# Attention followed by a two-layer product: another order of the first two units' start

## The chip, the cores and the metric

The kernel runs on one core of one Trainium2 chip. The metric is the device time of one execution in microseconds; lower is better. A core has several engines that run beside one another, each with its own queue of instructions in program order: PE (TensorE, the matrix products), DVE (VectorE), ACT (ScalarE), POOL (GpSimd) and SP (SyncE, here only a queue for transfers). They wait for one another by semaphores. PE reads from the on-chip memory SBUF and writes into PSUM, eight banks of accumulators, from which DVE and ACT read.

## The reference

```python
scores = scale * q @ k.T          # 8 batches, 12 heads, 448 rows, 64 columns
attn = softmax(scores)            # with the row maximum taken off
x = attn @ v                      # heads put side by side: 3584 x 768
h = x @ w_in                      # 768 x 2048
g = maximum(0.01 * h, h)
out = g @ w_out                   # 2048 x 768
```

Inputs and output are float32. The kernel computes in bfloat16 with float32 accumulation, and leaves out the maximum, since the scores are small.

## The kernel before, in words

A unit is a pair of heads of one batch; there are 48. For each unit q and k are loaded, cast to bfloat16 (`cast`, into the buffer `qkb`), turned so that the head's columns lie on the partitions (`transposes` on PE, with a copy from PSUM into `qkT`), and multiplied to scores (`scores`). A unit's 448 keys are dealt with in four chunks of 112, so a unit has four calls of `scores`, each a pair of products (one for each head), and four calls of `expo`, the exponentials on ACT. `pv` multiplies the exponentials with v, one head at a time (16 small products), and divides by the sums on DVE; v carries a column of ones for them. `x_transposes` turns a unit's result for the big products.

Scores go to three PSUM slots of two banks each, in rotation (`next_slot`): a fourth score waits until the exponential of the first has read its slot. Everything else of this stage shares two banks, in rotation (`next_bank`).

The order is written out by hand. The program's order is each engine's order, and a scheduler doesn't change it. `first(u)` writes the order of the first six units (the first batch); after it, attention of later units is placed between the big products by a planner, which the change doesn't touch.

The start before: three loads on SP's queue (L217 to L219: k and q of unit 0, k of unit 1), in float32. All other loads go over POOL's queue and are cast to bfloat16 on the way. While the first two are under way, PE runs seven products of 128x512 on zeros (`warm_up`, L239), and DVE sets constants. k of unit 0 is cast by ACT and DVE together, one head each (`both`, L263), then q the same way. `transposes(0)` turns k first and q after it, in two tiles, each followed by five small products on zeros (`stay_warm`); ACT copies k out of PSUM, DVE copies q. Then DVE casts q and k of unit 1, and `first(0)` begins. In `first`, unit 0's and unit 1's fourth scores come late, after the next unit's transposes (unit 0) or between the two halves of unit 0's `pv` (unit 1). POOL casts v of unit 1 and everything from unit 3 on, by the lists in `supply`; its queue begins with the loads.

In the profile's rows L217 to L219 appear as L173 (the helper's line), casts as L190 (q, k) and L198 (v), L264 and L265 (unit 0's), `warm_up` as L241, `stay_warm` as L247, transposes as L301 and their copy as L305, scores as L319, exponentials as L331 and L334 (a unit's fourth chunk), `pv` as L362, L374 and L375, `x_transposes` as L389 and L390.

Of the kernel before, what the change touches and what calls it, by code (L numbers as in the profile page):

```python
# [16 lines left out]
def kernel(  # L17
# [48 lines left out]
    banks = [ps_g.tile([P, 4 * P], F32, name=f"g{i}") for i in range(2)]  # L66
# [7 lines left out]
    def next_bank():  # L74

        banks.reverse()
        return banks[1]
# [41 lines left out]
    h = h_pool.tile([P, MD, (KEEP + 1) * P], BF16, name="h")  # L119
    h_mix = h_pool.tile([P, MH, 2, P], BF16, name="hmix")  # L120
# [90 lines left out]
    def load_w(n=1):  # L211
        for _ in range(n):
            if w_steps:
                o, i = w_steps.pop(0)
                nc.gpsimd.dma_start(out=o, in_=i)

    load_one(0, 1, nc.sync)  # L217
    load_one(0, 0, nc.sync)
    load_one(1, 1, nc.sync)  # L219
    ident = const_pool.tile([P, P], BF16)  # L220
    make_identity(nc, ident)
# [6 lines left out]
    load_soft(5, 1, (2,))  # L228
    load_w(1)

    warm = h_mix.rearrange("p m c t -> p (m c t)")[:, :512]
    nc.vector.memset(warm, 0.0)

    word = const_pool.tile([P, 2], BF16)
# [2 lines left out]
    nc.scalar.copy(gate[:, :1], gate[:, 1:])  # L237

    def warm_up(n):  # L239
        for _ in range(n):  # L240
            nc.tensor.matmul(next_bank(), warm[:, :P], warm, start=True, stop=True)  # L241

    def stay_warm(n):

        ps = next_slot()
        for _ in range(n):
            nc.tensor.matmul(ps[:, 0, :P], warm[:, :P], warm[:, :P], start=True, stop=True)  # L247

    warm_up(7)
    nc.vector.memset(qkT_all.rearrange("p u i c s -> p u (i c s)")[:, :, 2 * S:2 * S + EP], 0.0)  # L250
    nc.vector.memset(v_old.rearrange("p u h so d -> p (u h so) d")[:, :, D:], 1.0)
    nc.vector.memset(e_all[:SC, :, EM:EM + EP], 0.0)
# [6 lines left out]
        nc.vector.memset(v_all[j * D:(j + 1) * D, :, 2 * KC + j, D:], 1.0)  # L259
    nc.vector.memset(e_all[:, :, EL:], 0.0)  # L260
    fast = nc.vector.tensor_copy

    def both(o, i):  # L263
        nc.scalar.copy(o[:, 0], i[:, 0])  # L264
        fast(o[:, 1], i[:, 1])  # L265

    cast(0, (1,), both)
    cast(0, (0,), both)


    x_t = {}
# [18 lines left out]
    def turn_tile(bank):  # L290
        bank = next_bank() if bank is None else bank
        return bank.bitcast(BF16)

    def transposes(u, bank=None):
        n = SC if u < HY else P
        t, flat = qkb[u % NB], qkT[u % NQ].rearrange("p i c s -> p (i c s)")[:, :2 * NSC * n]
        for parts in ((1,), (0,)) if u == 0 else ((0, 1),):
            tr = turn_tile(bank)[:, :2 * NSC * n].rearrange("p (i s) -> p i s", i=2)
            for i in parts:
                for so in range(NSC):  # L300
                    nc.tensor.transpose(tr[:, i, ts(so, n)], t[:n, i, so].rearrange("p h d -> p (h d)"), ident[:n, :n])  # L301
            if u == 0:
                stay_warm(5)
            at = slice(parts[0], parts[-1] + 1)
            (nc.scalar.copy if u == 0 and parts == (1,) else nc.vector.tensor_copy)(  # L305
                flat.rearrange("p (i s) -> p i s", i=2)[:, at], tr[:, at]
            )

    sc_t = {}

    def scores(u, c):
        ps = next_slot()
        t = qkT[u % NQ]
        sc_t[u, c] = ps
        if u < HY:
            t = t.rearrange("p i c s -> p (i c s)")
            for j in range(2):
                p = slice(j * D, (j + 1) * D)
                nc.tensor.matmul(ps[:, j, :S], t[p, S + c * SC:S + c * SC + P], t[p, :S], start=True, stop=True)  # L319
# [548 lines left out]
    def first(u):  # L868

        scores(u, 0)  # L870
        scores(u, 1)
        if u < 2:
            scores(u, 2)
        expo(u, 0)
        if u == 0:
            warm_up(1)
        expo(u, 1)
        if u >= 2:
            x_transposes(u - 2, next_bank())
        if u == 1:  # L880
            transposes(u + 1)
        if u >= 1:
            pv(u - 1, 0)
        if u > 1:
            scores(u, 2)
            scores(u, 3)
        if u != 1:
            transposes(u + 1)
        if u == 0:
            cast(2, (0, 1), fast)  # L890
            cast(0, (2,), fast)
# [12 lines left out]
    transposes(0)  # L904
    cast(1, (0, 1), fast)
    for u in range(HP):
        first(u)

# [78 lines left out]
    def turned(u):  # L987

        return u < to["pe"] or to["pe"] == NPE and u < to["turn"]
# [261 lines left out]
```

## Time and profile before

| | us |
|---|---|
| median of 3 runs (lowest, highest) | 377.68 (377.44, 377.75) |
| the profiled execution, its own time | 377.66 |
| its span, first to last instruction | 375.9 |
| PE busy | 369.2 (98%) |
| ACT busy | 259.7 (69%) |
| DVE busy | 256.7 (68%) |
| POOL busy | 190.6 (51%) |

The profile is one execution recorded by the hardware. A row of a timeline is: start, duration (both in us), engine, line, operation, what it writes and reads, the shape, how many instructions of the same kind were put together, and in brackets how long the engine had been idle before and which instruction ended that. "PEld" is PE's loading of weights, which overlaps its products. The end of a product is modelled: it includes the way through the array, so rows overlap, and the next row's start tells when the next product was issued. A row with several instructions begins with the first of them and lasts to the end of the last. The view of waits sums an engine's idle time by what it waited for: in total, how often, and the longest.

### The profile page before, as it was taken

How to read it: one execution, taken by the hardware profiler on the slowest of the kernel's cores; microseconds unless marked ns; L12 is line 12 of the kernel's file. 1: busy time of each engine (PE TensorE's matmuls, PEld its weight loads, DVE VectorE, ACT ScalarE, POOL GpSimd, SP SyncE). 2: the span in 40 equal slices, each digit the busy share in tenths (PEclk: the TensorE clock that was granted, in tenths of full speed). 3: DMA queues.
4: the chain of work that ended last, by engine and by line, in shares of the span. 5: the costliest groups of instructions: out<-in, count | busy, mean ns of one | idle time of the engine just before them, and what ended most of it. 6: DMA issues, size and time to landing. Idle time of an engine off the chain costs nothing.

```text
span 375.9 us, 10127 instructions
## 1 busy us (share of the span) xinstructions
PE 369.2 (98%) x4008; PEld 266.0 (71%) x4008; DVE 256.7 (68%) x559; ACT 259.7 (69%) x399; POOL 190.6 (51%) x376
## 2 busy tenths in 40 slices
PE   7899999999999999999999999999999999999996
PEld 4664658756698566996569966599665995679765
DVE  5665868778666867676676665875847775685754
ACT  6998895866768786758766587666787658626721
POOL 8976871985269969624488235792347020000000
PEclk9999999999999999999999999999999999999999
DMA  9999999999499966963969748798345740321123
GB/s 155 200 204 206 193 204 201 159 167 155 94 183 164 118 135 91 205 149 57 154 126 142 148 65 78 178 150 165 60 66 109 134 110 0 75 62 42 44 65 105
DMA packets 99920, 48.08 MB, mean 128 GB/s; under 512 B 64672, under 2 KB 96928, under 8 KB 99872
## 3 DMA queue, kind: packets, MB, share of 16 engines
q0 software_dynamic: 39600, 22.47, 44.4%
q1 hardware_dynamic: 60080, 24.84, 33.1%
q8 instruction: 31, 0.51, 0.6%
q14 instruction: 17, 0.14, 0.1%
q10 hardware_dynamic: 192, 0.12, 0.1%
HBM read 45.61 MB, written 11.01 MB: 151 GB/s over the span
## 4 chain that ended last, share of the span: by engine, by line
PE 96%; ACT 2%; DVE 1%; issue 0%; ACTq 0%
PE g L683 30%; PE g L548 14%; PE sc L548 14%; PE sc L322 7%; PE sc L350 6%; PE sc L319 4%; PE g L424 4%; PE sc L645 4%; PE sc L362 3%; PE g L821 2%; PE sc L343 2%; ACT e L331 2%; PE g L301 1%; PE g L362 1%; PE g L241 1%; PE sc L424 1%
## 5 line engine op out<-in xcount | busy, mean ns | idle before, releaser
L331 ACT ACTIVATE e<-sc 128x896 bf16<-128x896 f32 (+1 forms) x144 | 123.9, 930 | 30.4 <-PE sc L322 20.5
L683 PE MATMUL g<-w_out_sb,h 128*128 128x384 bf16 (+1 forms) x440 | 84.1, 326 | 0.0
L683 PEld LDWEIGHTS <-h 128*128 128x128 bf16 x592 | 54.3, 97 | 41.1 <-issue 10.8
L537 ACT ACTIVATE h<-c 128x512 bf16<-128x512 f32 (+1 forms) x72 | 43.1, 610 | 30.2 <-DVE c L563 12.4
L548 PEld LDWEIGHTS <-w_in_sb 128*128 128x128 bf16 x576 | 54.6, 98 | 5.8
L190 POOL COPY qkb<-fq 112x512 bf16<-112x512 bf16 x34 | 24.0, 705 | 43.5 <-DMA qkT<-qkb 34.5
L548 PEld LDWEIGHTS <-w_in_mix 128*128 128x128 bf16 x432 | 40.5, 98 | 3.7
L201 POOL COPY v<-fv 128x384 bf16<-128x384 bf16 x30 | 17.9, 596 | 44.2 <-PE sc L350 41.3
L688 DVE COPY o<-g 128x384 f32<-128x384 f32 x47 | 26.0, 553 | 13.6 <-PE g L683 13.5
L350 PE MATMUL sc<-v,e 128*128 128x65 bf16 x720 | 33.3, 194 | 0.0
L322 PE MATMUL sc<-qkT 64*128 64x448 bf16 (+1 forms) x210 | 32.8, 353 | 0.0
L350 PEld LDWEIGHTS <-e 128*128 128x128 bf16 x720 | 31.1, 98 | 1.3
L979 DVE RECIPROCAL rec<-sc 112x8 f32<-112x8 f32 x42 | 8.7, 207 | 33.9 <-PE sc L350 16.6
L980 DVE TENSOR_TENSOR x<-sc,rec 112x512 bf16<-112x512 f32 x42 | 29.0, 691 | 1.6 <-DVE rec L979 0.2
L548 PE MATMUL g<-xT,w_in_sb 128*128 128x256 bf16 (+1 forms) x216 | 28.5, 268 | 0.0
L548 PE MATMUL sc<-xT,w_in_sb 128*128 128x256 bf16 (+1 forms) x216 | 28.5, 268 | 0.0
L694 DVE TENSOR_TENSOR o<-o,g 128x384 f32<-128x384 f32 x39 | 21.5, 550 | 9.1 <-PE g L683 4.4
L343 PE MATMUL sc<-v,e 128*128 128x130 bf16 x120 | 26.5, 221 | 0.0
L649 DVE TENSOR_TENSOR o<-o,sc 128x192 f32<-128x192 f32 x39 | 13.7, 351 | 18.1 <-PE sc L645 18.1
L683 PE MATMUL g<-w_mix,h 128*128 128x384 bf16 x128 | 24.6, 327 | 0.0
L163 POOL DMA_DIRECT2D fv<-in_v_dram x32 | 20.1, 640 | 6.8 <-DMA fq<-in_q_dram 1.9
L683 PE MATMUL g<-w_mix,hmix 128*128 128x384 bf16 x112 | 21.7, 327 | 0.0
(149 smaller groups left out, 744.1 us busy)
## 6 DMA issues: line engine op xcount, KB each, us to landing
fq<-in_q_dram POOLq DMA_DIRECT2D x17, 224.0 KB, 5.7
w_out_sb<-in_moe_w_out_dram POOLq DMA_DIRECT2D x4, 768.0 KB, 13.2
out_dram<-o SPq DMA_DIRECT2D x7, 336.0 KB, 3.5
w_in_sb<-in_moe_w_in_dram POOLq DMA_DIRECT2D x2, 1152.0 KB, 12.9
out_dram<-o SPq DMA_DIRECT2D x7, 288.0 KB, 3.7
fk<-in_k_dram POOLq DMA_DIRECT2D x15, 128.0 KB, 6.0
fv<-in_v_dram POOLq DMA_DIRECT2D x15, 128.0 KB, 4.9
fk<-in_k_dram POOLq DMA_DIRECT2D x15, 96.0 KB, 6.1
```

The costliest lines, as they stand in the source:

```text
L163: nc.gpsimd.dma_start(out=t[p, :n, :, :so].rearrange("p u h so d -> p (u h) (so d)"), in_=(q, k, v)[x][b, hs, keys].rearrange("h (p so) d ...
L190: by(t[:SC, x].rearrange("p so h d -> p h so d"), f)
L322: nc.tensor.matmul(ps[:, j, :S].rearrange("p (so s) -> p so s", so=NSC), t[p, 1, c], t[p, 0, :, :SC], start=True, stop=True,)
L331: nc.scalar.activation(e[:, :, c, :], ps[:n, :, :S], AX.Exp, scale=scale)
L343: nc.tensor.matmul(ps, e[:, EM + qc * SC:EM + qc * SC + P], vt[:, 2 * KC:].rearrange("p j d -> p (j d)"), start=True, stop=False, skip_gro ...
L350: nc.tensor.matmul(ps[:, j * (D + 1):(j + 1) * (D + 1)], e[:, at:at + P], vt[:, j * KC + c], start=False, stop=(c == KC - 1), skip_group_c ...
L537: nc.scalar.activation(hs[:, m:m + 2, cols], x.rearrange("p (m t) -> p m t", m=2), AX.Prelu, alpha=0.01)
L548: nc.tensor.matmul(ps[:, j * nh:(j + 1) * nh], w[:, kk, ts(j, P)], x[:, kk], start=(first and j == 0 and kk == 0), stop=(kk == KH - 1), sk ...
L683: nc.tensor.matmul(ps[:, cols], x[:, m], w[:, m], start=(first and m == 0), stop=(m == MH - 1), skip_group_check=True,)
L688: by(o[:, at], ps[:, :NW])
L694: nc.vector.tensor_add(o[:, at], o[:, at], ps[:, :NW])
L980: nc.vector.tensor_mul(x, ps[:, :, :, :D], rec.to_broadcast([SC, 2, 2 * NP, D]))
```

## The change

- The loads of q and k of unit 0 change places on SP's queue.
- The warm-up on zeros is 26 products of 128x128 in place of 7 of 128x512, and the block of zeros is a quarter as wide. Between the first scores and the first slot's release there are 4 of them in place of 1 wide one.
- A new function `begin` casts, turns and copies unit 0. q first: DVE casts three of its four blocks, ACT the fourth, PE turns it in one tile. Of k, DVE casts the first block, ACT the other three; PE turns the first block alone in a tile of its own, then the other three in a third tile; DVE copies all three tiles. Two and three small products on zeros stand between.
- Of unit 0, the first chunk's scores use 112 columns of weights in place of 128, so that they read nothing of the second block.
- Unit 0's fourth scores come ahead of unit 1's transposes. Unit 1's fourth scores come ahead of both halves of unit 0's `pv`.
- Unit 1's k is cast before its q, and `transposes(1)` works in two tiles, k first, each with its own copy; unit 0's special case in `transposes` is gone.

```diff
+    load_one(0, 0, nc.sync)
     load_one(0, 1, nc.sync)
-    load_one(0, 0, nc.sync)
     load_one(1, 1, nc.sync)
...
-    warm = h_mix.rearrange("p m c t -> p (m c t)")[:, :512]
+    warm = h_mix.rearrange("p m c t -> p (m c t)")[:, :P]
...
     def warm_up(n):
-        for _ in range(n):
-            nc.tensor.matmul(next_bank(), warm[:, :P], warm, start=True, stop=True)
+        for x in range(n):
+            nc.tensor.matmul((next_bank() if x % 4 == 0 else banks[1])[:, :P], warm, warm, start=True, stop=True)
...
-    warm_up(7)
+    warm_up(26)
...
-    def both(o, i):
-        nc.scalar.copy(o[:, 0], i[:, 0])
-        fast(o[:, 1], i[:, 1])
-
-    cast(0, (1,), both)
-    cast(0, (0,), both)
...
-        for parts in ((1,), (0,)) if u == 0 else ((0, 1),):
+        for parts in ((1,), (0,)) if u == 1 else ((0, 1),):
...
+    def begin():
+
+        t, flat = qkb[0], qkT[0].rearrange("p i c s -> p (i c s)")
+
+        def turned(x, so):
+            tr = turn_tile(None)[:, :S]
+            for j in so:
+                nc.tensor.transpose(tr[:, ts(j, SC)], t[:SC, x, j].rearrange("p h d -> p (h d)"), ident[:SC, :SC])
+            at = slice(so[0] * SC, (so[-1] + 1) * SC)
+            return flat[:, x * S + at.start:x * S + at.stop], tr[:, at]
+
+        def copy(by, x, so):
+            by(t[:SC, x, so].rearrange("p so h d -> p h so d"), raw[0][x][:, :, so])
+
+        copy(nc.scalar.copy, 0, slice(3, 4))
+        copy(fast, 0, slice(0, 3))
+        copy(nc.scalar.copy, 1, slice(1, 4))
+        copy(fast, 1, slice(0, 1))
+        one = turned(0, range(NSC))
+        stay_warm(2)
+        fast(*one)
+        one = turned(1, range(1))
+        stay_warm(3)
+        fast(*one)
+        one = turned(1, range(1, NSC))
+        fast(*one)
...
+                n = SC if u == c == 0 else P
+                nc.tensor.matmul(ps[:n, j, :S], t[p, S + c * SC:S + c * SC + n], t[p, :S], start=True, stop=True)
...
         if u == 0:
-            warm_up(1)
+            warm_up(4)
+            scores(u, 3)
...
         if u == 1:
             transposes(u + 1)
+            scores(u, 3)
...
-        if u < 2:
-            scores(u, 3)
...
-    transposes(0)
-    cast(1, (0, 1), fast)
+    begin()
+    cast(1, (1, 0), fast)
```

More of the change, by code (lines that the diff above doesn't have):

```diff
@@ L246, in stay_warm @@
         for _ in range(n):
-            nc.tensor.matmul(ps[:, 0, :P], warm[:, :P], warm[:, :P], start=True, stop=True)
-    warm_up(7)
+            nc.tensor.matmul(ps[:, 0, :P], warm, warm, start=True, stop=True)
+    warm_up(26)
     nc.vector.memset(qkT_all.rearrange("p u i c s -> p u (i c s)")[:, :, 2 * S:2 * S + EP], 0.0)
@@ L301, in transposes @@
                     nc.tensor.transpose(tr[:, i, ts(so, n)], t[:n, i, so].rearrange("p h d -> p (h d)"), ident[:n, :n])
-            if u == 0:
-                stay_warm(5)
             at = slice(parts[0], parts[-1] + 1)
-            (nc.scalar.copy if u == 0 and parts == (1,) else nc.vector.tensor_copy)(
-                flat.rearrange("p (i s) -> p i s", i=2)[:, at], tr[:, at]
-            )
+            nc.vector.tensor_copy(flat.rearrange("p (i s) -> p i s", i=2)[:, at], tr[:, at])
+    def begin():
[20 more added lines that the diff above has]
+        fast(*one)
+        raw[0].clear() if len(raw[0]) == 2 else [raw[0].pop(x) for x in range(2)]
     sc_t = {}
@@ L318, in scores @@
                 p = slice(j * D, (j + 1) * D)
-                nc.tensor.matmul(ps[:, j, :S], t[p, S + c * SC:S + c * SC + P], t[p, :S], start=True, stop=True)
+                n = SC if u == c == 0 else P
+                nc.tensor.matmul(ps[:n, j, :S], t[p, S + c * SC:S + c * SC + n], t[p, :S], start=True, stop=True)
             return
```

## The prediction

> **What bounds the kernel now.** I read the page first, then PE's list of waits, then each engine's timeline over the first 26 us, because the whole change lies there.
>
> ```profile
> span 375.9 us, 10127 instructions
> PE 369.2 (98%) x4008; PEld 266.0 (71%) x4008; DVE 256.7 (68%) x559; ACT 259.7 (69%) x399; POOL 190.6 (51%) x376
> PEclk9999999999999999999999999999999999999999
> ```
>
> ```profile
> PE g L241 <- DVE gate L236: 1.2, 1, 1.2
> PE sc L319 <- DVE qkT L305: 0.6, 2, 0.4
> PE sc L319 <- ACT e L331: 0.6, 3, 0.2
> PE sc L319 <- ACT c L334: 0.4, 1, 0.4
> PE g L389 <- DVE x L375: 0.3, 1, 0.3
> ```
>
> These waits sum to 3.1 us, and the last of them ends at 21.99 (row below). From there PE has no recorded wait. A shift of PE's position at 22 us is therefore worth its full size at the end, and nothing after 22 us can give more. Before it, ScalarE's exponentials set the pace:
>
> ```profile
> 3.59 0.40 ACT L264 CAST qkb<-w_in_mix 112x256 bf16<-112x256 f32 x1 [1.36 <-DMA w_in_mix<-in_k_dram]
> 4.30 0.41 ACT L264 CAST qkb<-w_in_mix 112x256 bf16<-112x256 f32 x1 [0.31 <-DMA w_in_mix<-in_q_dram]
> 6.53 2.53 ACT L331 ACTIVATE e<-sc 112x896 bf16<-112x896 f32 x3 [1.22 <-PE sc L319]
> ...
> 12.92 2.59 ACT L331 ACTIVATE e<-sc 112x896 bf16<-112x896 f32 x3
> ...
> 16.11 2.63 ACT L331 ACTIVATE e<-sc 112x896 bf16<-112x896 f32 x3
> ```
>
> The first exponential starts at 6.53, the ninth (unit 2) at 12.92, the thirteenth (unit 3) at 16.11, with no idle bracket between: 9.58/12 = 0.80 us each. One lasts 2.53 - 2 x 0.80 = 0.93 and frees its slot at its end. So the question is how much earlier the first starts, and whether PE can follow that.
>
> **The start, term by term.** PE and VectorE before:
>
> ```profile
> 1.20 3.17 PE L241 MATMUL g<-hmix 128*128 128x512 bf16 x7 [1.20 <-DVE gate L236]
> 4.16 0.58 PE L301 MATMUL g<-ident,qkb 112*128 112x112 bf16 x4
> 4.53 0.74 PE L247 MATMUL sc<-hmix 128*128 128x128 bf16 x5
> 5.06 0.58 PE L301 MATMUL g<-ident,qkb 112*128 112x112 bf16 x4
> 5.44 0.60 PE L247 MATMUL sc<-hmix 128*128 128x128 bf16 x5
> 6.13 0.74 PE L319 MATMUL sc<-qkT 64*128 64x448 bf16 x6
> ```
>
> ```profile
> 0.87 0.27 DVE L232 MEMSET hmix<- 128x256 uint32 x1 [0.87 <-PEq L1235]
> ...
> 3.59 0.29 DVE L265 CAST qkb<-w_in_mix 112x256 bf16<-112x256 f32 x1 [0.27 <-DMA w_in_mix<-in_k_dram]
> 4.24 0.29 DVE L265 CAST qkb<-w_in_mix 112x256 bf16<-112x256 f32 x1 [0.36 <-DMA w_in_mix<-in_q_dram]
> 5.68 0.39 DVE L305 COPY qkT<-g 128x448 bf16<-128x448 bf16 x1 [1.15 <-PE g L301]
> 6.49 0.29 DVE L190 COPY qkb<-w_in_mix 112x512 bf16<-112x512 bf16 x1 [0.41 <-DMA w_in_mix<-in_q_dram]
> 6.70 0.74 DVE L190 CAST qkb<-w_in_mix 112x512 bf16<-112x512 f32 x1
> ...
> 9.39 0.29 DVE L190 COPY qkb<-w_in_mix 112x512 bf16<-112x512 bf16 x1 [0.42 <-DMA w_in_mix<-in_k_dram]
> 10.00 0.47 DVE L198 COPY x_mix<-w_in_mix 112x512 bf16<-112x512 bf16 x1 [0.32 <-DMA w_in_mix<-in_v_dram]
> 10.90 0.62 DVE L305 COPY qkT<-g 128x896 bf16<-128x896 bf16 x1 [0.43 <-PE g L301]
> ```
>
> Loads: the same three issues on SP's queue with the first two exchanged, equal in bytes, so q lands where k did (3.59) and k where q did (4.24); unit 1's k stays third. Cost nothing.
>
> Warm-up: five 128-column products take 5.06 - 4.53 = 0.53, 0.106 each at the starting pace. 26 of them take 2.76 against 2.96 (1.20 to 4.16) for the seven wide ones. The memset is a quarter as wide: between 0.07 and 0.27, I take 0.10, so PE starts near 1.03 and is through at 3.8 (4.0 at the other end). That is hidden by q's cast.
>
> q's cast: VectorE does 384 elements; the nearest rows are 0.29 for 256 and 0.74 for 512. I take 0.44 (0.29 x 1.5), done at 4.03; ends 0.29 and 0.74. ScalarE's 128 elements (under the 0.40 of 256) end before. q's turning, four transposes 0.37 apart (4.16 to 4.53), issues 4.07 to 4.44 with its end at 4.65; two stay-warm products to 4.65.
>
> k: its first chunk (128 elements, 0.15 to 0.29, I take 0.20) is cast at 4.44, hidden; it is turned at 4.65, then three products to 5.06. ScalarE casts the other 384 elements from 4.30, at most 0.61 (0.41 x 1.5), to 4.91. VectorE copies q 4.67 to 5.06 (0.39) and the first chunk by about 5.25. The other chunks take the bank that q's copy has just read, so they wait to 5.10; three transposes end their issue at 5.38, and the first scores, which need only the first chunk, go at 5.38 instead of 6.13. Behind that bank wait stand all later scores, but nothing earlier is possible for them.
>
> From first scores to first exponential is 0.40 before (6.13 to 6.53). The second L247 group takes 0.60 against 0.74 for the same five, and a pair of scores follows the next by 0.19: PE doubled its pace near 5.8, though PEclk shows 9 throughout. At 5.38 the pair would be on the slow pace, 0.19 more. First exponential: 5.38 + 0.59 = 5.97, a gain of 0.56. Both ends: with the 0.29 cast and the full pace it gains 0.9; with the 0.74 cast at the slow pace, 0.26.
>
> [...]
>
> **The first two units.** The fourth scores of unit 0 now stand ahead of unit 1's transposes on PE, behind the first exponential's slot (5.97 + 0.93 + 0.05 = 6.95). They delay unit 1's k transposes, but its casts are due only with the loads (q seen at 6.49) and end by 7.44 at the latest (6.70 + 0.74), as before. Unit 1 could keep its old time and still be early enough: its first scores went at 8.58 and are needed at 5.97 + 3.19 = 9.16, with 0.40 between. Its extra half copy on VectorE (two of 0.39 for one of 0.62, 0.16 more) lies in the same gap. Cost nothing. The narrower first score (112 columns of weights) changes no time, since 448 columns still stream.
>
> ```profile
> 8.58 0.36 PE L319 MATMUL sc<-qkT 64*128 64x448 bf16 x2 [0.42 <-DVE qkT L305]
> ...
> 10.22 0.57 PE L301 MATMUL g<-ident,qkb 112*128 112x112 bf16 x8
> 10.62 0.26 PE L362 MATMUL g<-x_mix,e 112*128 112x65 bf16 x3
> ...
> 12.18 0.55 PE L319 MATMUL sc<-qkT 64*128 64x448 bf16 x4
> 12.98 0.37 PE L389 MATMUL g<-ident,x 112*128 112x112 bf16 x4 [0.25 <-DVE x L375]
> 13.19 0.26 PE L362 MATMUL g<-x_mix,e 112*128 112x65 bf16 x3
> ...
> 15.57 0.55 PE L319 MATMUL sc<-qkT 64*128 64x448 bf16 x4 [0.20 <-DVE qkT L305]
> ...
> 21.99 0.55 PE L319 MATMUL sc<-qkT 64*128 64x448 bf16 x4 [0.20 <-ACT e L331]
> ```
>
> Here absolute times come in. Unit 2's k lands at 9.39, so its transposes go at 9.73 at best (before 10.22). v of unit 0 lands at 10.00 and is cast by 10.47, so unit 0's first products go at 10.51 (before 10.62). What helps is the moved fourth score of unit 1: it leaves the place between the two halves of unit 0's products, where the half took from 10.62 to 11.57, and now stands ahead of the landing. The second half then waits for unit 2's copy (10.40 + 0.62, so 11.06) and ends its issue at 11.57; unit 2's scores go at about 11.68, 0.50 earlier than 12.18, and the turning of unit 0's result at 12.48.
>
> ```profile
> 9.65 0.72 POOL L163 DMA_DIRECT2D w_mix<-in_q_dram  x1 [0.77 <-DMA w_in_mix<-in_k_dram]
> 10.36 0.70 POOL L163 DMA_DIRECT2D w_mix<-in_k_dram  x1
> 11.06 1.17 POOL L190 COPY qkb<-w_in_mix 112x512 bf16<-112x512 bf16 x2
> 12.16 1.17 POOL L198 COPY x_mix<-w_in_mix 112x512 bf16<-112x512 bf16 x2
> ```
>
> The next term is a new wait. Unit 1's products, at 13.19 before and possible at 12.68 for PE, need its v, cast by POOL as the first of the pair at 12.16: 12.16 + 0.61 = 12.77, seen by PE about 0.05 later. POOL's queue is not moved: it hangs on the landing at 9.39, two DMA issues and two casts. So PE gains 13.19 - 12.82 = 0.37 there and no more. From 13.19 to 15.57 PE has one idle piece, the 0.20 behind unit 3's copy, which comes with its transposes; so unit 3's scores go at 15.20, and their exponential can start at 15.20 + 0.40 = 15.60. ScalarE would be ready at 5.97 + 9.58 = 15.55. The later one, 15.60, against 16.11: a gain of 0.51. From there both move together to 21.99, where PE takes over.
>
> **Sum.** The profiled execution took 377.66, its span 375.9 and 1.76 around it; the median of the runs is 377.68, 0.02 off. 377.66 - 0.50 = 377.16.
>
> **Rivals.** A, the gain of the start passes whole: POOL's cast comes sooner or its wait binds less. For it: the start could gain up to 0.9. Against it: four POOL rows back to back behind a landing that the change doesn't touch. At the full pace and my casts, 0.75: 376.91.
>
> B, the change does little: q's cast on VectorE takes the 0.74 of the wide row and the pace is slow, the start gains 0.26: 377.40. For it: the 0.74 row has the same pattern of columns; against it: 256 elements took 0.29 beside the same POOL work.
>
> [...]
>
> [...]
>
> **How the numbers follow.** My forecast (gain 0.35 to 0.65) 0.55, A 0.20, B 0.14, C 0.11. The bound of no change is 0.2% of 377.68, about what a measurement of this kernel can tell: 376.92 to 378.44. Faster than that needs A at its upper half, 0.13, and I add 0.02 for what I don't see. Slower needs C to last past 13 us, 0.05. The rest, 0.80, is the same. The range takes in A's 0.85 and the zero of B: 376.8 to 377.8; the likeliest case alone is 377.0 to 377.3.
>
> **What would show it.** Right: first exponential near 5.97 on ScalarE's timeline; first transposes near 4.07; PE at unit 1's products with a wait on POOL's copy, near 12.82; the thirteenth exponential near 15.6 after a short idle of ScalarE; no PE wait after 22 us. Wrong: POOL's v copy well before 12.16; PE's transposes still 0.09 apart after 7 us; a first exponential after 6.3; or a wait of PE for a load after 22 us, which would mean that loads, not PE, had been just in time.

## The result, and the profile after

The changed kernel takes 378.31 us, median of 22 runs (377.34 to 379.61); the kernel before, beside it, 377.66 (376.93 to 378.12, 22 runs). The ratio is 1.0022, 95% interval 1.0012 to 1.0031: slower by 0.2%, where 377.16 was predicted, with 376.8 to 377.8 as the range. A ratio weighs all the runs compared, so it need not be the quotient of the two medians. In the experiments two executions in a slow state are left out, one of before at 469.53 us and one of before_early14 at 749.5. Two things are in these 22 times. Eight of them lie above 379.0, none of before's does; and the other fourteen have their middle at 378.04, 0.38 above before's median. The profiled execution, 378.31, belongs to the fourteen.

The page's line with PE's busy time and its count of products:

```profile
PE 368.9 (98%) x4025; PEld 267.0 (71%) x4025; DVE 256.1 (68%) x562; ACT 259.6 (69%) x398; POOL 189.1 (50%) x376
```

ScalarE's timeline at the start:

```profile
5.82 2.53 ACT L349 ACTIVATE e<-sc 112x896 bf16<-112x896 f32 x3 [0.92 <-PE sc L337]
...
9.55 2.53 ACT L349 ACTIVATE e<-sc 112x896 bf16<-112x896 f32 x3 [0.39 <-PE sc L337]
...
16.09 2.53 ACT L349 ACTIVATE e<-sc 112x896 bf16<-112x896 f32 x3
```

The first exponential comes 0.71 sooner (5.82 for 6.53), the fifth 0.18 (9.55 for 9.73), the thirteenth 0.02 (16.09 for 16.11). What is gained on the first unit is given back on the next two. VectorE's and PE's timelines say where:

```profile
3.69 0.36 DVE L310 CAST qkb<-w_in_mix 112x384 bf16<-112x384 f32 x1 [0.58 <-DMA w_in_mix<-in_q_dram]
...
7.51 0.43 DVE L190 CAST qkb<-w_in_mix 112x512 bf16<-112x512 f32 x1 [1.68 <-DMA w_in_mix<-in_k_dram]
...
9.81 0.29 DVE L190 COPY qkb<-w_in_mix 112x512 bf16<-112x512 bf16 x1 [0.52 <-DMA w_in_mix<-in_k_dram]
...
10.49 0.39 DVE L198 COPY x_mix<-w_in_mix 112x512 bf16<-112x512 bf16 x1 [0.39 <-DMA w_in_mix<-in_v_dram]
```

```profile
4.11 0.56 PE L305 MATMUL g<-ident,qkb 112*128 112x112 bf16 x4 [0.16 <-DVE qkb L310]
...
5.38 1.05 PE L337 MATMUL sc<-qkT 64*112 64x448 bf16 x6
...
9.14 0.74 PE L337 MATMUL sc<-qkT 64*128 64x448 bf16 x6 [0.58 <-DVE qkT L296]
...
12.07 0.55 PE L337 MATMUL sc<-qkT 64*128 64x448 bf16 x4
12.89 0.37 PE L407 MATMUL g<-ident,x 112*128 112x112 bf16 x4 [0.27 <-DVE x L393]
13.25 0.25 PE L380 MATMUL g<-x_mix,e 112*128 112x65 bf16 x3
...
21.88 0.55 PE L337 MATMUL sc<-qkT 64*128 64x448 bf16 x4 [0.20 <-ACT e L349]
```

GpSimd's copies of v, of which unit 1's is the first:

```profile
12.58 1.16 POOL L198 COPY x_mix<-w_in_mix 112x512 bf16<-112x512 bf16 x2
```

Unit 1's first load is seen at 7.51 (its k; before it was q, at 6.49, and k no later than 6.70), unit 2's k at 9.81 (9.39), unit 0's v at 10.49 (10.00). At 21.88 PE stands 0.11 ahead of before's 21.99, where 0.50 was predicted. That is a smaller gain, and still no loss. In this execution the loss comes later, at one place. PE of before and of the changed kernel, 72 to 81 us (unit 14, the first that DMA transposes have turned):

```profile
72.50 0.74 PE L319 MATMUL sc<-qkT 64*128 64x448 bf16 x6
73.17 1.80 PE L683 MATMUL g<-w_out_sb,h 128*128 128x384 bf16 x10
...
76.17 0.81 PE L683 MATMUL g<-w_mix,h 128*128 128x384 bf16 x4
...
79.78 0.74 PE L319 MATMUL sc<-qkT 64*128 64x448 bf16 x6
```

```profile
72.39 0.55 PE L337 MATMUL sc<-qkT 64*128 64x448 bf16 x4
73.26 0.36 PE L337 MATMUL sc<-qkT 64*128 64x448 bf16 x2 [0.32 <-DMA qkT<-qkb]
73.56 1.80 PE L701 MATMUL g<-w_out_sb,h 128*128 128x384 bf16 x10
...
76.83 0.81 PE L701 MATMUL g<-w_mix,h 128*128 128x384 bf16 x4
...
80.49 0.74 PE L337 MATMUL sc<-qkT 64*128 64x448 bf16 x6
```

PE is 0.11 early at 72.39 and loses that in two steps: behind the wait for unit 14's DMA transposes it is 0.39 late (73.56 for 73.17), and at the products of w_mix 0.66 late (76.83). It is 0.71 late at 80.49, and stays so to the end. GpSimd's timeline of the two kernels over the same stretch:

```profile
64.19 1.01 POOL L190 COPY qkb<-fq 112x512 bf16<-112x512 bf16 x1 [8.16 <-DMA fq<-in_q_dram]
...
73.28 0.67 POOL L190 COPY qkb<-fq 112x512 bf16<-112x512 bf16 x1
...
74.94 1.12 POOL L190 COPY qkb<-fq 112x512 bf16<-112x512 bf16 x1
```

```profile
65.15 1.02 POOL L190 COPY qkb<-fq 112x512 bf16<-112x512 bf16 x1 [8.03 <-DMA fq<-in_q_dram]
...
73.99 0.67 POOL L190 COPY qkb<-fq 112x512 bf16<-112x512 bf16 x1
...
75.65 1.12 POOL L190 COPY qkb<-fq 112x512 bf16<-112x512 bf16 x1
```

GpSimd waits over 8 us for unit 14's q. From there on it runs copies and DMA issues with one short gap, for k (0.16 and 0.21), and its copies at 73 us begin 0.71 later than before, the same 0.71 as PE's. The DMA transposes that PE waits for at 73.26 read what GpSimd's first copies write. How the copies at 73 us and PE's second step hang together shows in VectorE's rows, of before and then of the changed kernel:

```profile
74.03 1.56 DVE L701 TENSOR_TENSOR h<-h 128x1024 bf16<-128x1024 bf16 x1 [1.60 <-PE g L683]
75.52 0.55 DVE L688 COPY o<-g 128x384 f32<-128x384 f32 x1
```

```profile
74.42 1.88 DVE L719 TENSOR_TENSOR h<-h 128x1024 bf16<-128x1024 bf16 x1 [1.78 <-PE g L701]
76.23 0.54 DVE L706 COPY o<-g 128x384 f32<-128x384 f32 x1
```

VectorE's difference of `h` ends 0.65 after the start of GpSimd's long copy (75.59 after 74.94, 76.30 after 75.65), whenever it began itself, and the copy to `o` behind it frees the bank that PE needs at 76.17 (76.83). Both rows are long there: the difference takes 1.56 and 1.88, against 0.69 at 77.75 in before, where GpSimd runs no copy beside it, and GpSimd's copy takes 1.12, against 0.66 to 0.67 for the three ahead of it. The same difference takes 0.69 us in before_keep and 0.83 in after_early14 (below), where the next copy to begin is the long one, and 2.11 in one_turn, where two more copies begin ahead of the long one. How the two come to lengthen each other the rows don't show.

### The profile page after: what moved, and what is told of

Its sections match the earlier page's. It is cut to its first block, busy times and chain, and to the rows that moved or that the text cites. A ratio compares the mean times of both kernels' runs of the same rounds, so it can differ in the third digit from the quotient of the medians.

```text
span 376.5 us, 10160 instructions
## 1 busy us (share of the span) xinstructions
PE 368.9 (98%) x4025; PEld 267.0 (71%) x4025; DVE 256.1 (68%) x562; ACT 259.6 (69%) x398; POOL 189.1 (50%) x376
## 4 chain that ended last, share of the span: by engine, by line
PE 87%; DMA 8%; DVE 1%; POOL 1%; issue 0%; ACT 0%; POOLq 0%; ACTq 0%
PE g L701 30%; PE g L566 14%; PE sc L566 14%; PE sc L340 7%; PE sc L368 6%; DMA fk<-in_k_dram 5%; PE sc L663 4%; PE sc L337 3%; PE g L442 2%; PE sc L380 2%; PE sc L361 2%; DMA w_in_mix<-in_v_dram 2%; DMA qkT<-qkb 2%; PE g L380 1%; PE g L294 1%; PE sc L442 1%
## 5 line engine op out<-in xcount | busy, mean ns | idle before, releaser
L201 POOL COPY v<-fv 128x384 bf16<-128x384 bf16 x30 | 16.0, 532 | 42.8 <-PE sc L368 39.9
```

## The experiments

Each time stands beside before's on the same chip. "Shift" is PE's position against before's profile, minus where PE is early.

**Is it the order of the loads?** swap_only changes only that in before: q of unit 0 is loaded, cast, turned and copied first.

```diff
-    load_one(0, 1, nc.sync)
     load_one(0, 0, nc.sync)
+    load_one(0, 1, nc.sync)
...
-    cast(0, (1,), both)
     cast(0, (0,), both)
+    cast(0, (1,), both)
...
-        for parts in ((1,), (0,)) if u == 0 else ((0, 1),):
+        for parts in ((0,), (1,)) if u == 0 else ((0, 1),):
...
-            (nc.scalar.copy if u == 0 and parts == (1,) else nc.vector.tensor_copy)(
+            (nc.scalar.copy if u == 0 and parts == (0,) else nc.vector.tensor_copy)(
```

> The kernel before, with only unit 0's loads exchanged (q ahead of k) and the casts, transposes and copies of unit 0 exchanged with them, so that nothing else differs. Theory L (the load order pushes the following loads back): unit 1's k is seen near 7.5 instead of 6.3, POOL waits for a load near 7.2, the q of unit 12 is seen near 65 instead of 64.2, PE waits at unit 14's first scores, and the time is 0.4 to 0.9 us above before. Theory V (landings vary by themselves from one execution to the next, and the changed kernel only has more of it for another reason): time within 0.2 us of before, and landings like those of before.

377.93 against 377.63, ratio 1.0007 (0.9998 to 1.0017). Its profile has unit 1's first load at 7.99, the changed kernel's had 7.51. But one_turn (below), with the changed order too, has it at 6.37, and before_keep, the same instructions as before up to 74 us, at 7.10 where before's profile has 6.49 (q in all of these but the changed kernel). So it varies by 0.6 us between two executions of the same instructions, and by 1.6 over these kernels; the order of the loads isn't shown to matter.

**Parts of the change undone.** late_scores puts the fourth scores of units 0 and 1 back; one_turn casts unit 1's q first and turns it in one tile; wide_warm takes the old warm-up of 512 columns.

```diff
             warm_up(4)
-            scores(u, 3)
...
             transposes(u + 1)
-            scores(u, 3)
...
+        if u < 2:
+            scores(u, 3)
         expo(u, 2)
```

> The changed kernel, with the fourth scores of units 0 and 1 put back to their old places. Theory S (the moved scores make PE idle ahead of unit 1 and cost the loss): back to before's time, 0.6 us below the changed kernel. Theories L and V: the loss at unit 14 stays, so the same time as the changed kernel within 0.3 us.

```diff
-        for parts in ((1,), (0,)) if u == 1 else ((0, 1),):
+        for parts in ((0, 1),):
...
-    cast(1, (1, 0), fast)
+    cast(1, (0, 1), fast)
```

> The changed kernel, with unit 1 cast q first and turned in one tile with one copy, as before. Theory T (unit 1's k first makes VectorE wait for the load that lands last): unit 1's scores come sooner and the time falls by up to 0.3 us. Theories L and V: as the changed kernel within 0.3 us, since the loss is at unit 14.

```diff
-    warm = h_mix.rearrange("p m c t -> p (m c t)")[:, :P]
+    warm = h_mix.rearrange("p m c t -> p (m c t)")[:, :512]
...
-        for x in range(n):
-            nc.tensor.matmul((next_bank() if x % 4 == 0 else banks[1])[:, :P], warm, warm, start=True, stop=True)
+        for _ in range(n):
+            nc.tensor.matmul(next_bank(), warm[:, :P], warm, start=True, stop=True)
...
-    warm_up(26)
+    warm_up(7)
...
-            warm_up(4)
+            warm_up(1)
```

> The changed kernel, with the old warm-up (7 products of 128x512, then 1) in place of the 26 and 4 of 128x128. Theory W (more and smaller instructions at the start, or PE at the slow pace, make the loss): back to before's time, and a spread of runs as narrow as before's 1.2 us. Theories L and V: as the changed kernel, near +0.6 us with a spread of 2 us; the first exponential may start 0.15 later (warm-up through at 4.16 instead of 3.95).

late_scores 378.34 (ratio 1.0021, 1.0011 to 1.0031), one_turn 378.57 (1.0031, 1.0020 to 1.0042), wide_warm 377.63 (1.0000, 0.9991 to 1.0009). Of these three, only the wide warm-up brings the time back to before's. one_turn shows more: in its profile (377.54, the lowest of its seven runs) PE is 0.57 early at 22 us and 0.59 early at 72 us, and this is what comes next (PE, then VectorE, then GpSimd):

```profile
71.91 0.80 PE L337 MATMUL sc<-qkT 64*128 64x448 bf16 x6
...
76.14 0.81 PE L701 MATMUL g<-w_mix,h 128*128 128x384 bf16 x4 [0.33 <-DVE o L706]
```

```profile
73.51 2.11 DVE L719 TENSOR_TENSOR h<-h 128x1024 bf16<-128x1024 bf16 x1 [1.35 <-PE g L701]
```

```profile
73.30 0.66 POOL L190 COPY qkb<-fq 112x512 bf16<-112x512 bf16 x1
...
74.97 1.12 POOL L190 COPY qkb<-fq 112x512 bf16<-112x512 bf16 x1
```

GpSimd's copies begin at 73.30, 0.02 from before's; VectorE's difference begins half a microsecond earlier than before's and ends at 75.62 all the same; PE's 0.59 is gone. A start that is better by more than half a microsecond is worth nothing in this execution.

wide_warm's profile shows the same at another place. PE is 0.24 early at 22 us and 0.37 late from 40.24 on, behind VectorE's `x`, which follows the mixing of w_in, which waits for w_in's landing (PE, then VectorE):

```profile
40.24 0.36 PE L337 MATMUL sc<-qkT 64*128 64x448 bf16 x2 [0.44 <-DVE x L998]
```

```profile
37.60 0.56 DVE L491 TENSOR_TENSOR w_in_mix<-w_in_sb 128x768 bf16<-128x768 bf16 x1 [3.59 <-DMA w_in_sb<-in_moe_w_in_dram]
```

In before's profile that row of VectorE stands at 36.63, and PE has no gap behind it.

**Combinations.** half_warm has 13 and 2 products of 256 columns for the 26 and 4; turn_wide is wide_warm with one_turn, turn_half is half_warm with one_turn.

```diff
-    warm = h_mix.rearrange("p m c t -> p (m c t)")[:, :P]
+    warm = h_mix.rearrange("p m c t -> p (m c t)")[:, :2 * P]
...
-            nc.tensor.matmul((next_bank() if x % 4 == 0 else banks[1])[:, :P], warm, warm, start=True, stop=True)
+            nc.tensor.matmul((next_bank() if x % 2 == 0 else banks[1])[:, :2 * P], warm[:, :P], warm, start=True, stop=True)
...
-    warm_up(26)
+    warm_up(13)
...
-            warm_up(4)
+            warm_up(2)
```

> The changed kernel, with 13 and 2 warm-up products of 256 columns in place of 26 and 4 of 128: the same columns in the same time at the start, but 30 PE instructions fewer, so 4 more than before. Theory I: the transposes land in 3.9 to 4.8 us, the loss at unit 14 is gone, and the median is 0.5 to 0.8 us below the changed kernel, at before's or a little under it. Rival P: as the changed kernel, 0.6 us above before.

> The changed kernel with the old wide warm-up and with unit 1 cast q first and turned in one tile: 10 PE instructions fewer than before. Theory I with the loads' path as the floor at unit 14: PE is 0.3 to 0.6 us ahead of before at 22 us, the transposes land in 3.9 to 4.8 us, and the median is 0 to 0.4 us below before. Without theory I (unit 1's turning or the loads make the loss): above before by 0.6 or more, as the same kernel with the narrow warm-up was.

> The changed kernel with 13 and 2 warm-up products of 256 columns and with unit 1 cast q first and turned in one tile: 4 PE instructions more than before, the earliest start tried. Theory I: 0.9 us below the same kernel with the narrow warm-up (378.57), at 377.4 to 377.7. Rival P: as that kernel.

half_warm 378.01 (1.0004, 0.9991 to 1.0017), turn_wide 377.82 (0.9998, 0.9985 to 1.0011), turn_half 377.40 (0.9996, 0.9983 to 1.0008): none is faster than before by more than its interval. turn_half's profiled execution took 378.62, and its stages show why (the columns are PE, weight load, VectorE, ScalarE and GpSimd busy, the granted clock, the DMA share and GB/s):

```profile
8.00:10.00 2.00, 1.17 (x12) 0.52 (x10) 0.92 (x2) 1.97 (x3) 0.69 (x1) 1.00 1.36 181
10.00:12.00 2.00, 1.31 (x19) 1.06 (x20) 1.28 (x3) 2.00 (x4) 1.67 (x4) 0.80 1.45 195
12.00:14.00 2.00, 2.00 (x28) 1.24 (x25) 1.22 (x4) 0.73 (x2) 2.00 (x4) 0.50 1.45 195
14.00:16.00 2.00, 2.00 (x34) 1.51 (x33) 1.00 (x3) 2.00 (x3) 2.00 (x5) 0.84 1.30 210
```

PE was busy for 1.17 of the 2 us from 8 to 10 and 1.31 of the next 2, was then granted less of the clock (0.80, 0.50 and 0.84 over 2 us each; if it was half or full, that makes 0.8 + 2 + 0.64, an estimate of some 3.4 us at half), and stood 1.16 late at 22 us. PE at the slow pace is what rival C, with 0.11, stands for. half_warm's profile has the best start of all, 0.68 early at 22 us; 0.48 of it goes at 39.68, at the same wait for VectorE's `x` as in wide_warm (w_in seen at 37.04), and from 74 us on PE is over a microsecond late, after 1.28 of waiting for unit 14's DMA transposes (GpSimd's wait for q ended at 66.03). half_warm and turn_wide miss what was expected of them.

**Is it PE's fetch of instructions?** The page's queue of instructions has 31 packets and 0.51 MB, so 16 KB each, and PE has 8050 rows (4025 products and as many weight loads; 8016 before), so a packet for some 260 of them; that the packets are PE's is my estimate from these counts. In the changed kernel 200 to 296 of PE's rows begin from one packet to the next, 261 from the one at 61.7 us to the one at 71.1. The change gives PE 34 rows more. The packet at 71.1 us (71.2 in before) stands 4.0 us behind the issue of the DMA transposes of units 14 and 15, and those land 5.7 us after issue (median of two); in before it is 5.1 and 4.3. extra17 adds 17 products of 8 columns to before:

```diff
+        if u == 1:
+            for _ in range(17):
+                nc.tensor.matmul(banks[0][:, :8], warm[:, :P], warm[:, :8], start=True, stop=True)
         scores(u, 0)
```

> The kernel before, with nothing but 17 products of 8 columns on zeros put on PE ahead of unit 1's first scores, where PE idles; with their weight loads 34 PE instructions more, as many as the change adds. Theory I (the changed count of PE instructions moves a 16 KB block of PE's instruction fetch into the transposes of units 14 and 15 near 70 us, which then land about 1.3 us later): the two transposes take 5.2 to 6.2 us to land instead of 3.9 to 4.7, PE loses 0.4 to 0.7 at unit 14, and the median is 0.5 to 0.9 us above before, with a spread like the changed kernel's. Rival P (the narrow products at the start themselves, by PE's pace or what they do to the loads): no change beyond 0.2 us, since the start is before's.

378.10 against 377.79 (1.0011, 1.0000 to 1.0021), the transposes landing after 5.7 us, shift +0.09 at 22 us and +0.58 from 79.78 on. At the time I read this as the cause. The landing does go with the fetch: in 14 profiles whose transposes were issued between 66 and 69 us, those with the fetch 4.7 us or more behind the issue landed after 4.0 to 4.4 us (seven; an eighth, at 4.9, after 5.1), and those with it sooner, 3.7 to 4.2 us, after 4.7 to 5.8 (six). plus32 and plus64 (below) have it sooner still: at 3.3 they landed after 5.0, at 2.3 after 4.4, and the last doesn't fit. But the landing isn't what holds PE in extra17: it runs through the transposes' scores without a gap, and stands at the bank, as late_scores does (0.30):

```profile
76.70 0.81 PE L683 MATMUL g<-w_mix,h 128*128 128x384 bf16 x4 [0.28 <-DVE o L688]
```

If the transposes were the cause all the same, the loss should go where they are early, so the next four kernels issue the loads of q and k of units 14 and 15 ahead of w_out's last two pieces: before, the changed kernel, turn_half, and turn_half with two products of 256 columns ahead of unit 1's scores (fill_early14).

```diff
-            load_w({9: 1, 10: 3}.get(g, 0))
+            load_w({9: 1, 10: 1}.get(g, 0))
+            if g == 10:
+                ahead = max(ahead, HP + 8)
+                fetch(2)
+                load_w(2)
```

> The kernel before, with the loads of units 14 and 15's q and k issued ahead of w_out's last two pieces. If in before the DMA transposes of unit 14 are just in time (issued at 66.10 us, the first scores of unit 14 without a wait), starting them earlier gains nothing: 377.4 to 377.9. The transposes should be issued before 65 us. Against it: w_out's last pieces land some 2 us later, and VectorE's mixing of w_out waits: then 378 or more.

> The changed kernel with the same edit of the loads. If the changed kernel's loss at 73 us is the late landing of the DMA transposes, it goes (transposes issued before 65 us, no wait of PE for them), and PE's shift against before at 22 us, -0.1 in the profiled run, holds to the end: 377.2 to 377.7, 0.6 to 1.0 under the changed kernel. If the narrow products of the warm-up cost by themselves, it stays at 378.0 to 378.6.

> The changed kernel with a warm-up of 256 columns, unit 1 turned in one tile and the same edit of the loads. If the transposes of unit 14 are the floor under a start that is 0.3 to 0.7 sooner, it now passes whole: 376.8 to 377.3. If something after unit 14 is the floor, 377.4 to 377.8.

> The last one with two more products of 256 columns ahead of unit 1's scores, where PE stands idle. They run while PE waits for a load, so they cost nothing in a common execution: within 0.2 of the last kernel. If the runs of 378.6 to 379.6 come from PE's idle time between 8 and 10 us, fewer of its runs lie above 378.5 than the two in twelve without these products.

378.14 (1.0006, 0.9992 to 1.0020), 377.96 (1.0015, 0.9999 to 1.0030), 378.03 (1.0014, 0.9998 to 1.0031), 377.71 (1.0000, 0.9986 to 1.0013), against 377.75; turn_half_early14 is above both of the ranges given for it. The transposes were out of the way, some 7 us sooner, and PE waits for none of them. Yet fill_early14, 0.26 early at 72 us, is at 0.00 at 77.72. What holds it is the cost that before_early14's expectation names: w_out's last pieces land later, VectorE mixes them later, and `x` is late (PE, then VectorE):

```profile
73.01 0.36 PE L337 MATMUL sc<-qkT 64*128 64x448 bf16 x2 [0.22 <-DVE x L1001]
```

```profile
66.60 0.56 DVE L454 TENSOR_TENSOR w_mix<-w_out_sb 128x768 bf16<-128x768 bf16 x1 [2.92 <-DMA w_out_sb<-in_moe_w_out_dram]
...
72.27 0.69 DVE L1001 TENSOR_TENSOR x<-sc,rec 112x512 bf16<-112x512 f32 x1
```

VectorE sees w_out at 66.60 in fill_early14, 66.69 in turn_half_early14, 66.92 in after_early14 and 67.79 in before_early14; `x` follows 5.66 to 5.67 later in all four, and PE's shift at 80 us is 0.00, 0.09, 0.31 and 1.18. So these four put another limit in the way, and don't say whether the transposes alone had cost the changed kernel its time. The kernels with the loads of unit 14 and VectorE's order as they were, but for turn_half, plus32 and plus64, which are 1.1 to 2.5 us late at 72 us, stand as follows:

| kernel | PE's shift at 22 us | at 72.5 us | from 79.78 us on | copies at 73 us begin, against before |
|---|---|---|---|---|
| changed kernel | -0.11 | -0.11 | +0.71 | +0.71 |
| late_scores | +0.05 | +0.06 | +0.57 | +0.57 |
| extra17 | +0.09 | +0.09 | +0.58 | +0.58 |
| one_turn | -0.57 | -0.59 | +0.02 | +0.02 |
| turn_wide | -0.28 | -0.28 | +0.03 | +0.04 |
| half_warm | -0.68 | -0.20 | +1.12 | +1.88 |
| wide_warm | -0.24 | +0.37 | +0.23 | +0.58 |
| swap_only | +0.49 | +0.48 | +0.35 | +0.70 |

In the first five PE comes before VectorE's difference has ended beside GpSimd's long copy (the fourth of the row, 1.12), and ends up where GpSimd is, within 0.01. half_warm is held by the transposes instead. In wide_warm and swap_only, where PE is 0.37 and 0.48 late at 72.5 us, the long copy is the third of the row (1.13), one sooner; they end 0.14 and 0.13 under their own shift, as turn_half, plus32 and plus64 do (0.12 and 0.13), which come later still. before_keep, below, gains the same 0.14 and loses it again at 227 us.

**The wait behind GpSimd, moved.** The next four put VectorE's copy to `o` ahead of the difference of `h`, so that PE's bank no longer waits for both; fill_keep is fill_early14 with the loads in their old order.

```diff
+            if (i, c) == (0, 0):
+                keep(o1, left, b, idle if c == 0 and short else calm)
             for x in halves:
                 nc.vector.tensor_sub(h[:, x, one], h[:, x, two], h[:, x, one])
-                if x is halves[0]:
+                if x is halves[0] and (i, c) != (0, 0):
```

> The kernel before, with VectorE's first copy of a bank to o ahead of its difference of h in the first block (the same work, in the other order). In the profile of before PE has no gap there (the products of w_mix begin at 76.17 us, 0.01 after the ones before), so nothing is to be gained: 377.4 to 377.8. Below 377.2 would mean that before itself waited there.

> The changed kernel with the same order of the two. Its loss at unit 14 was 0.32 us for the transposes and the rest, some 0.4, for the bank behind the stretched difference. If that reading is right, the second part goes: 377.8 to 378.1, PE's shift against before at 76.9 us +0.2 to +0.4 where it was +0.66. If the transposes are the whole cause, no change: 378.1 to 378.5.

> The changed kernel with the wide warm-up and unit 1 turned in one tile (377.82, PE 0.28 early at 22 us and 0.02 early after unit 14), and the same order of the two. If VectorE behind GpSimd's copies is the floor there, the 0.28 now passes: PE's shift at 76.9 us -0.2 to -0.3, 377.3 to 377.6. If not, the shift at 76.9 us stays at 0.0 and the time at 377.7 to 377.9.

> The changed kernel with a warm-up of 256 columns, unit 1 turned in one tile, two products of 256 columns ahead of unit 1's scores, the loads in their old order, and the same order of the two. Its rows of PE, 4012, are 3 more than before's 4008 and one, so the fetch of PE's instructions should stand near 71 to 72 us as in before, clear of the transposes. If the two floors at unit 14 are all that held the gain, 376.9 to 377.4, under before; if a third one stands behind them, 377.5 to 377.9.

377.63 (1.0002, 0.9994 to 1.0011), 378.16 (1.0012, 1.0002 to 1.0021), 377.61 (1.0006, 0.9993 to 1.0020), 378.19 (1.0016, 1.0007 to 1.0025), against 377.60. turn_wide_keep keeps its 0.27 over this place, the only one to do so, and loses it at the next (PE, and VectorE ahead of it):

```profile
75.89 0.81 PE L701 MATMUL g<-w_mix,h 128*128 128x384 bf16 x4
...
77.43 0.36 PE L337 MATMUL sc<-qkT 64*128 64x448 bf16 x2 [0.23 <-DVE x L1000]
```

```profile
75.57 0.96 DVE L463 TENSOR_TENSOR w_out_sb<-w_out_sb 128x768 bf16<-128x768 bf16 x1
...
76.68 0.69 DVE L1000 TENSOR_TENSOR x<-sc,rec 112x512 bf16<-112x512 f32 x1
```

The step of w_out's mixing, 0.55 in its short rows, takes 0.96 beside GpSimd's copies, `x` starts no sooner than in before (76.68 in both), its slot of scores comes free late, and the shift is 0.00 at 79.78. The wait was the right one; its removal moves the floor 3 us on, no further. after_keep and fill_keep don't test it: their profiled starts were late (+0.39 and +0.21 at 22 us), and that passed to the end (+0.34 and +0.27). Their medians lie over what was expected if the reading is right.

**More small products.** plus64 and plus32 add 64 and 32 small products to the changed kernel, to move the fetch away from the transposes, or leave it among them.

```diff
+    def tiny(n):
+        for _ in range(n):
+            nc.tensor.matmul(banks[0][:, :8], warm, warm[:, :8], start=True, stop=True)
...
-    warm_up(26)
+    warm_up(20)
+    tiny(21)
...
     def first(u):

+        tiny((0, 17, 12)[u] if u < 3 else 0)
...
+        if u == 0:
+            tiny(20)
         if u != 1:
             transposes(u + 1)
```

(plus32 has the 21, and 17 ahead of unit 1's scores.)

> The changed kernel with 64 more products on zeros (six of the 26 of 128 columns become 21 of 8, and 17, 12 and 20 of 8 columns stand ahead of unit 1's and 2's scores and unit 1's turning, where PE waits). 128 more rows of PE: fetches come every 9.7 us for 256 rows here (61.5 and 71.1), so the one at 71.0 goes to about 66. If its place among the transposes (issued 3.9 us before it) is the cause, the two transposes land 4.0 to 4.4 us after their issue, PE does not wait for them, and the time falls to 377.5 to 378.0. If the narrow products cost by themselves, it stays at 378.3 or rises.

> The same with 32 more products (21 of 8 columns for six of the 26, and 17 ahead of unit 1's scores): the fetch goes to about 68.6, 1.5 to 2.5 us after the transposes' issue, among them still. By the first theory they land 4.7 to 6 us after their issue and the time stays at 378.0 to 378.6. If the time goes with the number of products alone, it lies between the changed kernel's and that with 64.

380.15 (1.0066, 1.0053 to 1.0080) and 378.76 (1.0025, 1.0012 to 1.0037). Of PE's loss at unit 14 they can't tell, since the added products hold up the start: plus64 is 2.54 late already at 22 us, and loses nothing at unit 14 then (+2.41 at the end). But PE's rows in plus64 are the clearest on its pace:

```profile
8.96 0.91 PE L299 MATMUL g<-ident,qkb 112*128 112x112 bf16 x8
...
10.51 1.30 PE L342 MATMUL sc<-qkT 64*128 64x448 bf16 x6
...
13.52 0.33 PE L385 MATMUL g<-x_mix,e 112*128 112x65 bf16 x3
...
13.71 0.26 PE L385 MATMUL g<-x_mix,e 112*128 112x65 bf16 x3
```

Eight transposes take 0.91 where they take 0.57 at full pace, six scores 1.30 for 0.74, until 13.6 us, 12.6 us after PE started, although PE was busy for 5.89 of the 6 us from 8 to 14. In this execution PE was occupied, by products of 8 columns in part, and the pace did not come.

## Why the prediction was wrong

- **The first exponential** (0.56 sooner, ends 0.26 and 0.9): 0.71, inside. First transposes at 4.11 (near 4.07 said), first scores at 5.38 (5.38 said); q's cast took 0.36 for the 0.44 taken. The pair of scores with 112 columns of weights took 0.40 (5.38), one with 128 took 0.37 (6.79).
- **"Cost nothing" for unit 1, by the landings of before's profile**: failed, in its inputs. Unit 1's first load, 6.49, 7.10 in before_keep, which runs the same instructions, was 7.51 here and 7.99 in swap_only. One profile gives one landing out of several (6.37 to 7.99 over these kernels), and a term of 0.5 us can't be built on it. With 7.51 unit 1's scores came at 9.14, against 8.58. The 9.16 I had is when the fifth exponential could start, 0.40 behind its scores, so 8.76 was the last harmless time; ScalarE stood idle for 0.39 ahead of the fifth, and 0.53 of the 0.71 was gone (0.18 left). Then unit 2's k and unit 0's v were 0.42 and 0.49 late, and 0.02 was left at the thirteenth.
- **The new wait for GpSimd's copy of v** (12.82): right in its mechanism, wrong in its time. GpSimd's copies hang on unit 2's k, as I had it, and began at 12.58 for 12.16, 0.42 late like that landing. With 0.61 for the first, 12.58 + 0.61 = 13.19, and PE's products went at 13.25, against 13.19 before. The four turnings ahead of them began at 12.89 and were 0.21 in before; here 0.36 passes, so about 0.15 is the wait, too short for a bracket. The gain of 0.37 I had there is a loss of 0.06.
- **"From there PE has no recorded wait. A shift of PE's position at 22 us is therefore worth its full size at the end"**: this is the step that decides, and it failed. A list without a wait doesn't say how much room there is. In before, PE reaches unit 14 just when GpSimd and VectorE do: one_turn, 0.57 early at 22 us, ended 0.02 late, and the changed kernel, 0.11 early, 0.71 late. At 39 us it is the same with VectorE behind w_in's landing (half_warm, 0.68 early, 0.20 after it). Where PE came later than GpSimd, its delay passed but for some 0.13 (plus64, swap_only); no profile shows a gain at 22 us that passed. I had named the sign of it ("loads, not PE, had been just in time"), and gave it no chance of its own.
- **Rivals.** A's price of 0.75 and B's of 0.26 fall with that step, since both carry the start's gain to the end. C, with 0.11, is PE still at the slow pace past 11.2 us, because its early work now has gaps; that gaps hold it there was assumed, and no run shows it. In the changed kernel's profile the pace doubled near 4.5 us (products of 128 columns 0.10 apart at 4.46, 0.06 at 4.74), sooner than before's 5.8, and after 7 us its transposes are 0.05 apart (eight in 0.57 at 7.99), where 0.09 was the sign of C. Where a slow pace was seen PE was 1.16 late at 22 us (turn_half) and 2.54 (plus64, where the added products' own time is in it). I counted PE's full pace in before (eight transposes in 0.57 at 10.22) as evidence against C; it is evidence on a warm-up of 512 columns.
- **The high runs.** Runs above 378.8 us: 20 of 65 in the kernels with the 26 products of 128 columns (the changed kernel, late_scores, one_turn, after_early14, after_keep), 10 of 58 in those with 256 columns (half_warm, turn_half, turn_half_early14, fill_early14, fill_keep), 4 of 36 where the wide ones are put back (wide_warm, turn_wide, turn_wide_keep), none of before's 22 beside the changed kernel and 2 of its 166 in all. The mean granted clock of each execution bears on what these are. turn_half's profiled execution, which lost the clock for some 3.4 us, has 0.995; so have two of the changed kernel's eight above 379.0 (379.39 and 379.61), and five of the 20, against none of the 45 others. The other six read 1.00, as plus64 does although its rows are at the slow pace. So for two of the eight a lapse of the clock is on record, and for six it stays argued; there is no profile of the changed kernel in such an execution. fill_early14, with two products where PE idles, has one of 11 runs above 378.5, turn_half_early14 without them five of 12, which points the same way and is too little to decide.
- **Slips in the working**: "A's 0.85 and the zero of B" in the range are not the 0.75 and 0.26 worked out for them, and the sum takes 0.50 for the 0.51 ahead of it. Neither changes the outcome.

In the profile the 0.71 comes from GpSimd's wait for unit 14's q, which ended at 65.15 for 64.19. The DMA engines are busy until then (nine tenths or more in every slice from 5 us on), and had moved less by 64 us (the DMA view of before, then of the changed kernel, 0 to 64 us):

```profile
DMA packets 16770, 12.45 MB, mean 195 GB/s; under 512 B 1965, under 2 KB 16761, under 8 KB 16761
```

```profile
DMA packets 16229, 12.18 MB, mean 190 GB/s; under 512 B 1947, under 2 KB 16220, under 8 KB 16220
```

0.27 MB at 195 GB/s is 1.4 us, more than the 0.96. before_keep had 12.31 MB by then and its wait ended at 64.94, with PE where it is in before to 0.01 us, so this too varies between executions of the same instructions. Over the sixteen profiles without early loads the wait ends between 64.16 and 66.03, and before's is near the early end. So before's profile was a lucky one to compare with, and part of the 0.71 is that luck and not the change.

Over all runs, one part of the change is shown to cost: the narrow warm-up. Ratios of the five kernels with the 26 products are 1.0012 to 1.0031; with the wide ones put back (wide_warm) the time is before's, 1.0000 (0.9991 to 1.0009), and seven other kernels with 512 or 256 columns have 0.9996 to 1.0016, of which only fill_keep's, the highest, is clear of 1. Part of that cost is the high runs. What the rest is, the 0.38 between the two middles, stays open: extra17, with the same count of PE's rows as the changed kernel and the wide warm-up, had 0.31 (interval 0.00 to 0.79), and which property of the added rows does it wasn't isolated. No kernel here was faster than before by more than its interval.

## What to carry to other kernels

An engine that is 98% busy with no recorded wait can still be just in time: before a gain is carried from the start to the end, find the first stage where another queue (here VectorE behind w_in's landing at 37 us, and GpSimd behind 64 us of loads) has been waiting for something that the gain doesn't move, and compare its rows there with PE's. A landing read off one profile is one draw; a term under a microsecond built on it needs a second profile of the same kernel. And a warm-up is to be judged on many runs, by the runs that lie high: here 20 of 65 with the narrow one against 4 of 36 with the wide one.

## What the runs showed of the hardware

- VectorE's difference of 128x1024 took 0.69 us at the least and 2.11 beside a row of GpSimd's copies, and in nineteen of the twenty profiles (all but plus64's) it ended 0.60 to 0.68 us after the start of the one copy that was stretched (1.08 to 1.15 for 0.61 to 0.67).
- In turn_half the granted clock was 0.80, 0.50 and 0.84 over the three stretches of 2 us from 10 us on (an estimate of some 3.4 us at half), after PE had been busy for 1.17 of the 2 us from 8 us and 1.31 of the next 2. In plus64, with products of 8 columns among the others, eight transposes took 0.91 for 0.57 and six scores 1.30 for 0.74, until 13.6 us, 12.6 after PE's start, with PE busy for 5.89 of the 6 us from 8 to 14. There the granted clock reads 1.00 all along, so the pace has to be read from the rows. What sets the pace isn't shown.
- A packet of the instruction queue (16 KB, one for some 260 of PE's rows by the counts) stood 3.7 to 4.2 us behind two DMA transposes' issue in six profiles, and those landed 0.3 to 1.8 us later than the 4.0 to 4.4 of seven with the packet 4.7 to 5.1 us behind. An eighth, at 4.9, landed after 5.1, and plus64, at 2.3, after 4.4, so the cause isn't shown.
